# Head order, scaled maxima, the spatial product by seven products of halves, and a new order of pieces in an attention and gating kernel

## Chip, cores and metric

One Trainium2 chip, one core in use. The metric is the device time of one execution in microseconds (us), as the median of several runs. A profiled execution of the kernel before gives the span and the rows below.

## What is computed

```python
scores = concat(where(|i-j| < 16, q@k.T/8, -1e9), q@blockmax(k).T/8 + log(32))
a = softmax(scores);  x = a @ concat(v, blockmean(v))     # 2 batches, 8 heads, 768 x 64; blocks of 32
x = concat_heads(x)                                       # 2 x 768 x 512
gate = sigmoid(causal_conv5(x));  x = (gate * (x @ w_val)) @ w_out
h = relu(x @ w_in)                                        # 512 -> 1024
u, v = h[..., :512], h[..., 512:]
v = (v - mean) / sqrt(var + 1e-6)
out = (u * (w_spatial @ v + b_spatial)) @ w_out2
```

The weights of the last three lines and w_val arrive as 64-bit floats.

## The kernel before

Nearly all the work is fp32 matmuls. Each fp32 operand is held as a high and a low part, and `mm3` (396) multiplies high by high, high by low and low by high: three matmuls per product of 128 x 128 by 384 or 512 columns. The high part is a cast, mostly on ScalarE (ACT), the low part a subtraction, mostly on GpSimd (POOL); `WHO` (32) says which engine does which. `load64` (444) brings a 64-bit weight tile in: one DMA, one ACT `activation` into PSUM and two operations on VectorE (DVE: a shift and a shift-or). `split64` (462) then makes high and low. So each such tile of 128 x 512 costs ACT two instructions.

The program is a list of pieces that `ORDER` (42) names in sequence; a piece can call others that it needs:

- `lk`, `lq`, `lv`, `kw`, `vsum`, `put`: keys, queries, values, windows and block summaries of a pair of heads. `kw` takes the block maxima of the keys on DVE and copies the keys on ACT and POOL.
- `score`, `at`, `pv` (567 to 660), 16 ticks of two heads and half the sequence each. `scores` multiplies, takes minus the row maximum by `tensor_reduce` into `nm` in SBUF, scales `nm` by 0.125 in place, and has ACT do six exponentials with `nm` as bias. `a_T` transposes, and ACT copies into `aT`. `pv` multiplies with v; the two heads write to two halves of the columns of the array. Then ACT copies (`xhi`), DVE subtracts (`xlo`), and the convolution runs over the same PSUM bank: one ACT multiplication (`conv0`), four DVE multiply-adds.
- `gate` (663): one tanh per half sequence and batch (four gates in all). `val` (671): four products by w_val per gate, each followed by a DVE product with the gate, an ACT cast and a POOL subtraction, which give G.
- `wp` (783): w_out by w_in, worked out ahead of the rest in two halves; the weights for the first half are `wout` and `in1`, for the second `in0`.
- `v` (687): 128 rows of the v half, 12 matmuls of 512 columns, relu on ACT, the normalisation on DVE and POOL, high and low parts. `u` (717): the u half.
- `s` (735): the spatial product, 16 pieces (four per half sequence and batch) of 18 matmuls of 384 columns; DVE adds the bias from PSUM and multiplies by u, ACT casts, POOL subtracts. `ws` loads w_spatial.
- `r` (754): 128 rows of the result, 12 matmuls of 512 columns, one ACT copy, one DMA; the last row block goes in two halves of columns.

`Planner` (60) records every instruction of all pieces with what it depends on, sorts them by a table of costs, and issues them per engine in that sequence (`issue`). Every instruction is issued in one place, so the profile puts all on line 190; rows are told apart by the names of tiles (`u` any of 28 general buffers, `ps` PSUM, `a` the scores, `nm` the maxima) and their shapes. Each engine runs its list in sequence and waits at its head.

## Time and profile before

| | us |
|---|---|
| runs, median of 3 (lowest, highest) | 286.23 (285.75, 287.6) |
| the profiled execution, its own time | 283.49 |
| its span in the trace | 281.7 |
| busy: PE, DVE, ACT, POOL | 264.4, 172.9, 160.9, 132.6 |

PE is TensorE, whose granted clock stands at 1.00 in every window. A busy time sums the instructions of an engine; the ends of matmuls are modelled, and a matmul that is drawn longer than the next one's start still counts as busy. The trace shows two matmul records for each instruction of the scores and of the product with v. In a row of windows, the columns are: stretch, its length, then for PE, PEld (weight loads), DVE, ACT and POOL the busy us with the number of instructions, the granted clock, the share of the DMA engines, GB/s.

### The profile page before, as it was taken

What the parts mean: (1) busy time and instruction counts of PE and PEld (TensorE: products, weight loads), DVE (VectorE), ACT (ScalarE), POOL (GpSimd) and SP (SyncE); (2) the same over time, 40 slices, a digit from 0 to 9 for tenths busy, and PEclk for the clock granted to TensorE, in tenths of its full rate; (3) what the DMA queues carried; (4) which work ended last, traced back from release to release, by engine and by line L of the source; (5) the groups of instructions that cost most, each with busy time, mean ns of one, the idle gap of its engine ahead of it and who ended that gap; (6) DMA issues with size and microseconds to landing.
All of it is one profiled execution on the core that took longest, in us unless ns stands there. A gap on an engine that the chain in (4) does not pass through costs nothing.

```text
span 281.7 us, 5411 instructions
## 1 busy us (share of the span) xinstructions
PE 264.4 (94%) x1976; PEld 234.2 (83%) x1976; DVE 172.9 (61%) x394; ACT 160.9 (57%) x440; POOL 132.6 (47%) x166
## 2 busy tenths in 40 slices
PE   0599999999899999999999899999999999999995
PEld 0385677788788998889999889989899989999885
DVE  1897778789979992882489697927595401024000
ACT  3887989999797549869325867534364211211221
POOL 4797673615776275496602634058475500112100
PEclk9999999999999999999999999999999999999999
DMA  6999998889991113430000020002022031000222
GB/s 233 384 409 346 268 250 171 202 216 234 381 258 51 42 24 109 107 100 14 0 2 3 0 77 2 2 0 74 2 74 74 0 114 74 0 2 0 76 80 106
DMA packets 13466, 32.15 MB, mean 114 GB/s; under 512 B 1853, under 2 KB 4448, under 8 KB 13440
## 3 DMA queue, kind: packets, MB, share of 16 engines
q1 hardware_dynamic: 13248, 31.66, 37.3%
q8 instruction: 15, 0.25, 0.4%
q0 software_dynamic: 192, 0.15, 0.2%
q14 instruction: 11, 0.09, 0.1%
HBM read 27.48 MB, written 3.15 MB: 109 GB/s over the span
## 4 chain that ended last, share of the span: by engine, by line
PE 63%; ACT 13%; DMA 8%; DVE 7%; issue 4%; POOL 3%; POOLq 0%; ACTq 0%; DVEq 0%
PE ps L190 63%; ACT a L190 6%; ACT u L190 4%; DMA u<-in_moe_w_out_dram 4%; DVE u L190 3%; DMA u<-in_moe_w_spatial_dram 3%; POOL u L190 2%; ACT aT L190 2%; DMA u<-in_moe_w_in_dram 2%; DVE nm L190 1%; DVE a L190 1%; DVE km L190 1%; ACT ps L190 1%; POOL a L190 1%; DVE st L190 0%
## 5 line engine op out<-in xcount | busy, mean ns | idle before, releaser
L190 PE MATMUL ps<-u,u 128*128 128x384 f32 (+3 forms) x1452 | 232.4, 345 | 10.1 <-ACT u L190 8.9
L190 PEld LDWEIGHTS ps<-u,u 128*128 128x128 f32 (+1 forms) x1452 | 205.4, 200 | 29.8 <-ACT u L190 9.5
L190 POOL TENSOR_TENSOR u<-u,u 128x512 fp32r<-128x512 f32 (+2 forms) x70 | 86.1, 1245 | 90.5 <-ACT u L190 86.6
L190 ACT CAST u<-u 128x384 fp32r<-128x384 f32 (+2 forms) x70 | 39.7, 588 | 35.9 <-DVE u L190 29.8
L190 DVE SCALAR_TENSOR_TENSOR u<-ps,cw,u 128x384 f32<-128x384 f32 (+4 forms) x64 | 37.2, 607 | 1.3 <-ACT u L190 1.2
L190 ACT ACTIVATE u<-ps 128x512 fp32r<-128x512 f32 (+2 forms) x44 | 23.7, 566 | 24.3 <-PE ps L190 24.1
L190 POOL TENSOR_TENSOR a<-a,sm 128x360 f32<-128x360 f32 x32 | 25.7, 822 | 22.7 <-DVE sm L190 17.0
L190 DVE TENSOR_TENSOR gate<-ps,bias 128x384 f32<-128x384 f32 x16 | 8.6, 551 | 36.9 <-PE ps L190 36.9
L190 ACT ACTIVATE a<-a,nm 128x120 f32<-128x120 f32 x48 | 18.4, 393 | 4.9 <-DVE nm L190 3.9
L190 ACT COPY u<-ps 128x512 f32<-128x512 f32 (+1 forms) x13 | 7.2, 555 | 23.0 <-PE ps L190 23.0
L190 DVE TENSOR_SCALAR u<-u 128x512 uint32<-128x512 uint32 (+1 forms) x21 | 14.8, 712 | 8.0 <-DMA u<-in_moe_w_in_dram 5.3
L190 PEld LDWEIGHTS ps<-aT,u 120*64 120x64 f32 x384 | 14.2, 137 | 6.2 <-ACT aT L190 2.9
L190 PE MATMUL ps<-aT,u 120*64 120x64 f32 x384 | 16.1, 225 | 3.5 <-ACT aT L190 1.8
L190 ACT ACTIVATE a<-ps,nm 128x120 f32<-128x120 f32 x48 | 16.9, 362 | 1.4 <-DVE nm L190 0.4
L190 ACT ACTIVATE ps<-u 128x512 f32<-128x512 f32 x20 | 13.0, 650 | 7.9 <-DMA u<-in_moe_w_in_dram 4.0
L190 ACT COPY aT<-ps 120x384 f32<-120x384 f32 x32 | 13.8, 498 | 4.8 <-PE ps L190 4.8
L190 DVE SCALAR_TENSOR_TENSOR u<-ps,u 128x512 uint32<-128x512 uint32 x20 | 13.5, 685 | 1.9 <-ACT ps L190 1.1
L190 DVE BATCH_NORM_STATS2 st<-u 128x6 f32<-128x512 f32 x12 | 8.2, 685 | 10.3 <-ACT u L190 10.2
L190 DVE TENSOR_SCALAR sm<-ps 128x3 f32<-128x3 f32 x32 | 5.1, 158 | 15.2 <-ACT a L190 15.0
L190 PE MATMUL ps<-ident,a 128*120 128x128 f32 x96 | 13.6, 276 | 0.1
L190 PEld LDWEIGHTS ps<-ident,a 128*120 128x120 f32 x96 | 10.8, 137 | 1.8 <-issue 0.5
L190 DVE TENSOR_TENSOR u<-ps,u 128x384 fp32r<-128x384 f32 x16 | 8.6, 550 | 4.9 <-ACT u L190 3.4
(50 smaller groups left out, 184.5 us busy)
## 6 DMA issues: line engine op xcount, KB each, us to landing
u<-in_moe_w_in_dram SPq DMA_DIRECT2D x8, 512.0 KB, 9.8
u<-in_moe_w_out_dram SPq DMA_DIRECT2D x8, 512.0 KB
ks<-in_k_dram SPq DMA_DIRECT2D x8, 384.0 KB, 10.9
u<-in_q_dram SPq DMA_DIRECT2D x8, 384.0 KB
u<-in_vn_dram SPq DMA_DIRECT2D x8, 384.0 KB, 8.4
u<-in_v_dram SPq DMA_DIRECT2D x16, 192.0 KB, 4.7
out_dram<-u SPq DMA_DIRECT2D x11, 256.0 KB, 2.0
u<-in_moe_w_spatial_dram SPq DMA_DIRECT2D x6, 384.0 KB, 3.6
```

Of the source, the lines that this page charges most:

```text
L190: getattr(real, method)(*args, **kw)
```

## The change

1. `ORDER` is rewritten, and some of the planner's costs with it (start of the DMA wire, small bf16 matmuls, which DVE instructions share a port with POOL). A PSUM tile that two engines touch now makes a dependency whatever the addresses.
2. In `pv` each matmul depends on the copies of both heads.
3. The maxima go into spare PSUM columns of the score bank; the scaling reads them there and writes `nm`.
4. In `pv` ACT's reads of the bank are recorded ahead of DVE's.
5. Batch 1's spatial product is done by seven products of halves: the 768 x 768 and 768 x 512 operands are cut in halves, sums of halves are formed, and 14 pieces of nine matmuls of 384 columns take the place of eight of 18. w_spatial is loaded a second time (6 DMAs of 384 KB).
6. Code behind `KSC`, which is 0, goes.

```diff
 ORDER = """
-    in1 wout mask*2 wout in1 wp*2 wout in1 wp in1 in0 wout lk*2 wp in0 wval*2 in0*2 lk kw lk wp lq score vsum lq masks
...
+    mask*2 wout in1*4 wout cw wp*2 wout masks wout in0*3 lk lq wp*2 lq kw lk kw in0 lv vsum lk*2 score put lq kw score
...
-                if (w or writes) and a0 < p1 and p0 < a1 and b0 < f1 and f0 < b1:
+                if name.startswith("ps") and q.eng != eng:
+                    o.deps.add(q)
+                elif (w or writes) and a0 < p1 and p0 < a1 and b0 < f1 and f0 < b1:
                     o.deps.add(q)
...
+        raw = banks[0][:, NI * KW + NI : NI * KW + 3 * NI].rearrange("p (h i) -> p h i", h=2)
         for h in range(2):
-            dve.tensor_reduce(nm[:, h], s3[h], axis=AX.X, op=ALU.max, negate=True)
-        if not KSC:
-            dve.tensor_scalar(nm, nm, 0.125, None, op0=ALU.mult)
+            dve.tensor_reduce(raw[:, h], s3[h], axis=AX.X, op=ALU.max, negate=True)
+        dve.tensor_scalar(nm, raw, 0.125, None, op0=ALU.mult)
...
             copy("at", ATT[t, h], pt)
+            LAST[t, h] = plan.ops[-1]
...
+                    plan.ops[-1].deps.update((LAST[t, 0], LAST[t, 1]))
...
-        copy("xhi", xx[:, 0], x)
-        sub("xlo", xx[:, 1], x, f(xx[:, 0]))
         if g:
             act.copy(xp[:, 0:4], XL[n])
+        copy("xhi", xx[:, 0], x)
...
+        sub("xlo", xx[:, 1], x, f(xx[:, 0]))
         for s in range(1, 5):
...
+    def fast_v(t, h):
+        n = NT // 2
+        if t < n:
+            x = HX[t] = bass.AP(h.tensor, h.offset, [h.ap[0], [1, 768]])
+            dve.tensor_sub(x[:, 512:768], x[:, 256:512], x[:, 0:256])
+            hi, lo = th.get(), th.get()
+            copy("vhi", hi, x[:, 256:768])
+            sub("vlo", lo, x[:, 256:768], f(hi))
+        else:
+            x, y = HX.pop(t - n), bass.AP(h.tensor, h.offset, [h.ap[0], [1, 1280]])
+            dve.tensor_add(y[:, 512:768], x[:, 0:256], y[:, 0:256])
+            dve.tensor_sub(y[:, 768:1024], y[:, 512:768], x[:, 256:512])
+            dve.tensor_sub(y[:, 1024:1280], y[:, 256:512], y[:, 768:1024])
+            hi, lo = unit()[:, 0:1280], unit()[:, 0:1280]
+            copy("vhi", hi, y)
+            sub("vlo", lo, y, f(hi))
+        FV[t] = (hi, lo)
+
+    def fast_t(t):
...
+            sp.dma_start(raw[i], w_sp[(t + i * NT // 2) * P : (t + i * NT // 2 + 1) * P, :])
...
+        dve.tensor_sub(t1, b12, b11)
+        dve.tensor_sub(t2, b22, t1)
+        dve.tensor_sub(t3, b22, b12)
+        dve.tensor_sub(t4, b21, t2)
+        hi, lo = unit(), unit()
+        for i in range(2):
+            cs = slice(2 * i * CH, 2 * (i + 1) * CH)
+            copy("wshi", hi[:, cs], y[:, cs])
+            sub("wslo", lo[:, cs], y[:, cs], f(hi[:, cs]))
+        FT[t] = (hi, lo)
+
+    PRODUCTS = [(x, j) for x in (1, 6, 2, 7, 4, 5, 3) for j in range(2)]
...
+    def fast_s(i):
...
+            for k, (a, c) in enumerate(((0, 0), (0, 1), (1, 0))):
+                pe.matmul(po, A[a], Bs[c], start=first and t == 0 and k == 0, stop=t == n - 1 and k == 2, skip_group_check=True)
+        if x == 1:
+            y = SUM["p", j] = ps_.get().rearrange("p (a s) -> p a s", a=2)
+            for g in range(2):
+                dve.tensor_add(y[:, g], po, bias[:, g * CH : (g + 1) * CH])
+            SUM["e", j] = ps_.get().rearrange("p (a s) -> p a s", a=2)
+        elif x == 6:
+            dve.tensor_add(SUM["e", j][:, 0], po, SUM["p", j][:, 1])
+        elif x == 7:
+            dve.tensor_add(SUM["e", j][:, 1], po, SUM["p", j][:, 1])
+        if x in (1, 6, 7):
+            return
+        g, m, other = {2: (0, 2 + j, bias[:, 0:CH]), 4: (0, j, SUM["p", j][:, 0]), 5: (1, j, SUM["e", j][:, 1]), 3: (1, 2 + j, SUM["e", j][:, 0])}[x]
+        finish_s(b, g, m, po, other, f"f{i}")
```

`finish_s` holds the bias, u, cast and subtraction of the old `spatial`; the first three result blocks of batch 1 need ten of the 14 products, the last three all.

What the rewritten order does on SP, which issues the loads, from the ninth load on. Before:

```order
L190 DMA u_109<-in_moe_w_out_dram 128x1024
L190 DMA ks_78<-in_k_dram 128x768
L190 DMA ks_79<-in_k_dram 128x768
L190 DMA u_115<-in_moe_w_in_dram 128x1024
L190 DMA u_118<-in_moe_w_val_dram 128x1024
L190 DMA u_121<-in_moe_w_val_dram 128x1024
L190 DMA u_124<-in_moe_w_in_dram 128x1024
L190 DMA u_126<-in_moe_w_in_dram 128x1024
L190 DMA ks_80<-in_k_dram 128x768
L190 DMA u_133<-in_q_dram 128x768
L190 DMA u_140<-in_vn_dram 96x1024
L190 DMA u_141<-in_vn_dram 96x1024
```

After, from the sixth:

```order
L195 DMA u_97<-in_moe_w_out_dram 128x1024
L195 DMA u_105<-in_moe_w_out_dram 128x1024
L195 DMA u_109<-in_moe_w_out_dram 128x1024
L195 DMA u_112<-in_moe_w_in_dram 128x1024
L195 DMA u_115<-in_moe_w_in_dram 128x1024
L195 DMA u_118<-in_moe_w_in_dram 128x1024
L195 DMA ks_78<-in_k_dram 128x768
L195 DMA u_120<-in_q_dram 128x768 x2
L195 DMA ks_79<-in_k_dram 128x768
L195 DMA u_128<-in_moe_w_in_dram 128x1024
L195 DMA u_131<-in_v_dram 64x768 x2
L195 DMA u_131<-in_v_dram 16x1472 x2
```

Here `in_moe_w_out` and `in_moe_w_in` are weight tiles of 512 KB, `in_moe_w_val` those of w_val, `ks` a pair's keys, `in_q` its queries. The first keys stand at place 10 before and at 12 now, but the first queries move from place 18 to 13, and the w_val tiles behind the values. Counted over ACT's list, 14 activations and 14 casts of 64-bit tiles and three copies of keys stand ahead of the first exponential before, 12, 11 and two now.

On ACT, between the tanh of the first gate and the last of the four casts (`CAST u_<-u_ 128x384`) that make the high part of G. Before:

```order
L190 COPY ps_269<-xl_202 128x4
L190 CAST u_247<-u_177 128x384 x2
L190 CAST u_250<-u_177 128x384
L190 CAST u_245<-u_244 128x768
L190 COPY aT_266<-ps_265 120x384
L190 COPY aT_268<-ps_267 120x384
L190 CAST u_270<-u_244 128x768
L190 CAST u_242<-ps_269 128x384
L190 ACTIVATE u_243<-ps_269,cw 128x384
L190 ACTIVATE a_257,ps_253<-ps_253,nm_255 128x120 x3
L190 ACTIVATE a_258,ps_254<-ps_254,nm_255 128x120 x3
L190 CAST u_250<-u_177 128x384
```

And now:

```order
L195 COPY aT_247<-ps_246 120x384
L195 COPY aT_249<-ps_248 120x384
L195 CAST u_235<-u_182 128x384 x2
L195 CAST u_238<-u_182 128x384 x2
L195 COPY ps_268<-xl_181 128x4
L195 CAST u_269<-ps_268 128x384
L195 ACTIVATE u_270<-ps_268,cw 128x384
L195 COPY ps_271<-xl_200 128x4
L195 ACTIVATE a_254,ps_250<-ps_250,nm_252 128x120 x3
L195 ACTIVATE a_255,ps_251<-ps_251,nm_252 128x120 x3
L195 CAST u_269<-ps_271 128x384
```

The four casts stood apart, with two casts of w_spatial (128x768) and six exponentials ahead of the last; they now follow one another ahead of the exponentials. DVE's list moves alike: the four products of gate and val stood as three and one, and now stand together.

On PE, the tick of the product with v in which the heads did not take turns, in the stretch behind the first `v` piece (`aT_` numbers are heads; x6 is six in a row). Before:

```order
L190 MATMUL ps_435<-aT_410,u_228 64x64
L190 MATMUL ps_435<-aT_408,u_228 64x64
L190 MATMUL ps_435<-aT_410,u_228 64x64
L190 MATMUL ps_435<-aT_408,u_228 64x64
L190 MATMUL ps_435<-aT_410,u_228 64x64
L190 MATMUL ps_436<-aT_412,u_229 64x64 x6
L190 MATMUL ps_436<-aT_414,u_229 64x64 x6
L190 MATMUL ps_443<-u_245,u_280 128x384 x3
```

And now:

```order
L195 MATMUL ps_467<-u_440,u_222 128x384 x2
L195 MATMUL ps_448<-aT_445,u_442 64x64 x5
L195 MATMUL ps_448<-aT_447,u_442 64x64 x5
L195 MATMUL ps_448<-aT_445,u_442 64x64
L195 MATMUL ps_448<-aT_447,u_442 64x64
L195 MATMUL ps_464<-aT_461,u_442 64x64
L195 MATMUL ps_464<-aT_463,u_442 64x64
L195 MATMUL ps_464<-aT_461,u_442 64x64
```

One tick in that stretch keeps its heads apart in both orders (six and six before, five and five now); all others there take turns in both. Ahead of the first `v` piece 22 matmuls follow one of the same head before, two now.

## Rows read from the trace of the kernel before

**Rows 1.** Four windows (columns: stretch, us, busy us of PE, PEld, DVE, ACT, POOL).

```profile
28.20:62.60 34.40, 33.63 (x368) 25.31 (x367) 27.15 (x69) 31.89 (x115) 18.84 (x32) 1.00 0.91 222
62.60:88.40 25.80, 24.58 (x253) 22.02 (x251) 23.70 (x54) 21.87 (x70) 16.58 (x18) 1.00 0.91 257
88.40:170.50 82.10, 80.28 (x735) 74.81 (x733) 60.29 (x155) 51.95 (x160) 41.94 (x49) 1.00 0.14 41
170.50:278.70 108.20, 108.13 (x565) 99.52 (x564) 42.20 (x90) 35.33 (x67) 34.17 (x34) 1.00 0.12 43
```

**Rows 2.** Two more windows, same columns: to the second gate, and spatial stage.

```profile
5.30:97.90 92.60, 85.47 (x731) 68.81 (x732) 79.70 (x171) 77.81 (x223) 56.66 (x74) 1.00 0.86 252
207.00:249.00 42.00, 42.00 (x225) 39.62 (x224) 12.22 (x25) 12.67 (x24) 12.86 (x12) 1.00 0.16 57
```

**Rows 3.** Groups by form, PE, 170.5 to 278.7 us (count, busy, mean ns).

```profile
L190 PE MATMUL ps<-u,u 128*128 128x384 f32 x336 | 59.5, 335 | 0.1
L190 PE MATMUL ps<-u,u 128*128 128x512 f32 x204 | 47.2, 390 | 0.0
```

**Rows 4.** Timeline of ACT (start us, us, instruction, count [idle before]).

```profile
5.29 0.64 ACT L190 ACTIVATE ps<-u 128x512 f32<-128x512 f32 x1 [3.27 <-DMA u<-in_moe_w_in_dram]
...
33.75 0.35 ACT L190 ACTIVATE a<-ps,nm 128x120 f32<-128x120 f32 x1
...
74.54 0.83 ACT L190 CAST u<-u 128x768 fp32r<-128x768 f32 x1 [1.03 <-DMA u<-in_moe_w_spatial_dram]
...
80.51 0.52 ACT L190 CAST u<-u 128x384 fp32r<-128x384 f32 x1
...
270.41 0.59 ACT L190 COPY u<-ps 128x512 f32<-128x512 f32 x1 [2.13 <-PE ps L190]
273.13 0.59 ACT L190 COPY u<-ps 128x512 f32<-128x512 f32 x1 [2.13 <-PE ps L190]
```

**Rows 5.** Timeline of DVE: a scaling of maxima, and products of gate and val.

```profile
33.06 0.16 DVE L190 TENSOR_SCALAR nm<-nm 128x6 f32<-128x6 f32 x1
...
71.42 1.48 DVE L190 SCALAR_TENSOR_TENSOR u<-u,ps 128x384 f32<-128x384 f32 x3
...
79.83 0.55 DVE L190 SCALAR_TENSOR_TENSOR u<-u,ps 128x384 f32<-128x384 f32 x1
...
97.93 0.56 DVE L190 SCALAR_TENSOR_TENSOR u<-u,ps 128x384 f32<-128x384 f32 x1
```

**Rows 6.** Timeline of PE: the first v half, then products with v.

```profile
81.08 2.36 PE L190 MATMUL ps<-u,u 128*128 128x512 f32 x11
...
119.36 0.92 PE L190 MATMUL ps<-aT,u 120*64 120x64 f32 x24
...
154.98 2.31 PE L190 MATMUL ps<-aT,u 120*64 120x64 f32 x60
158.08 0.91 PE L190 MATMUL ps<-aT,u 120*64 120x64 f32 x12 [0.79 <-ACT aT L190]
```

**Rows 7.** Groups by form, whole span (count, busy us, mean ns).

```profile
L190 POOL TENSOR_TENSOR u<-u,u 128x512 fp32r<-128x512 f32 x32 | 43.1, 1355 | 27.5 <-ACT u L190 23.8 <-POOL u L190 1.8 <-DMA ks<-in_k_dram 1.7
...
L190 ACT CAST u<-u 128x512 fp32r<-128x512 f32 x32 | 19.6, 618 | 8.8 <-DVE u L190 8.5
...
L190 ACT ACTIVATE a<-ps,nm 128x120 f32<-128x120 f32 x48 | 16.9, 362 | 1.4 <-DVE nm L190 0.4
...
L190 ACT ACTIVATE ps<-u 128x512 f32<-128x512 f32 x20 | 13.0, 650 | 7.9 <-DMA u<-in_moe_w_in_dram 4.0 <-DMA u<-in_moe_w_out_dram 2.9 <-DMA u<-in_moe_w_val_dram 0.6
L190 POOL TENSOR_TENSOR u<-u,u 128x768 fp32r<-128x768 f32 x6 | 11.1, 1843 | 2.8 <-ACT u L190 2.7
...
L190 DVE TENSOR_TENSOR u<-gate,u 128x384 f32<-128x384 f32 x16 | 9.3, 594 | 0.5
...
L190 ACT COPY u<-ks 128x768 f32<-128x768 f32 x8 | 6.7, 842 | 2.0 <-POOL u L190 2.0
...
L190 DVE TENSOR_SCALAR nm<-nm 128x6 f32<-128x6 f32 x16 | 5.7, 357 | 0.0
```

More of the change, by code (lines that the diff above doesn't have):

```diff
@@ L171, in cost @@
             one = method in ("tensor_copy", "tensor_scalar") and not psum and not out_psum
-            lock = one or len(sbuf_in) > 1
+            lock = one or len(big) > 1 or n == 1 and not psum
             ptr = sum(1 for x in args[2:5] if hasattr(x, "ap") and size(x) == 1) if method != "tensor_tensor" else 0
@@ L733, in tile_kernel, with finish_s @@
     yh = Parts(768)
+    def finish_s(b, g, m, po, other, name):
+        yy = Y[b, g, m] = yh.get().rearrange("p (a s) -> p a s", a=2)
+        u = U[b, m][:, g * CH : (g + 1) * CH]
+        gt = att([P, CH], "gate", f"gate{name}")
+        dve.tensor_add(gt, po, other)
+        eng("ymul").tensor_mul(u, gt, u)
+        copy("yhi", yy[:, 0], u)
+        sub("ylo", yy[:, 1], u, f(yy[:, 0]))
     def spatial(i):
+        if i >= (B - 1) * NC * KT:
+            return fast_s(i - (B - 1) * NC * KT)
         (b, g), m = divmod(i // KT, NC), i % KT
@@ L839, in tile_kernel @@
         "wp": w_product(), "val": each(B * NC * KT, val), "v": each(B * NT, vhalf), "u": each(B * NC * KT, uhalf),
-        "ws": w_spatial(), "out2": split64("out2", w_out2, 0), "s": each(B * NC * KT, spatial), "r": each(B * NT, result)}
+        "ws": w_spatial(), "out2": split64("out2", w_out2, 0), "wt": each(NT // 2, fast_t), "s": each((B - 1) * NC * KT + 14, spatial), "r": each(B * NT, result)}
     count = {name: 0 for name in threads}
```

96 lines of the change are left out of this document (59 added, 37 removed).

## The prediction

> **What bounds the kernel now.** I read the windows first. In the last 108.2 us PE is busy for 108.13 and is never starved [rows 1]: there each matmul taken away is time taken away. From 88.4 to 170.5 it is busy for 80.28 of 82.1, from 28.2 to 88.4 for 58.2 of 60.2. This last figure flatters it, since a matmul that has to wait is drawn long. Counting pitch shows the starving: result blocks of 12 matmuls come 273.13 − 270.41 = 2.72 us apart [rows 4], 0.227 us per matmul of 512 columns. The 336 of 384 columns then share 108.2 − 204 × 0.227 = 61.9 us with the 25 others of that window [rows 1, 3]; as half of a 512 each, these take 2.8, which leaves 0.176 us per matmul of 384. Ahead of the first v half, which starts at 81.08 [rows 6], stand 104 matmuls of 512 columns (23.6 us by this pitch), 48 of 384 (8.4), six ticks of the product with v at 0.9 [rows 6], nine of scores, taken as long (together 13.5), and transposes and masks, which I estimate by their columns at 9: some 55 us. About 26 us of PE are lost there, and only some 5 behind it. Next I looked at who makes PE wait: from 28.2 to 62.6 ACT is busy for 31.89 of 34.4, from 62.6 to 88.4 DVE for 23.70 of 25.8 [rows 1]. So the head of the program is bound by the lists of ACT and DVE, the rest by PE.
>
> **The head, by the new order.** The same matmuls stand ahead of the first v half in both orders, by kind and count, so the change there is the waiting. ACT works through its list from 5.29, reaches the first exponential at 33.75 and the fourth cast of G at 80.51 [rows 4]; PE follows at 81.08.
> Ahead of the first exponential go two activations, three casts and a copy of keys: 2 × 0.650 + 3 × 0.618 + 0.842 = 4.0 us [rows 7]. A 20-wide operation that moves ahead takes back some 0.2. That is −3.8 us.
> From there to the fourth cast, six exponentials leave (at least 0.362 each, 2.2; with the read of the sum behind each, nearer 3), a cast of w_spatial (0.83 [rows 4]) and two casts and two multiplications of a PSUM bank (about 2.0, taken like the 0.52 of the last cast). In come two activations, three casts and two copies of keys, 1.3 + 1.85 + 1.68 = 4.8 us [rows 7]: the splits of w_val, which were only put off. Together −0.2 to −1; I take −1.
> So ACT gives −4.8 us at the first v half. DVE allows as much: its fourth product of gate and val starts 79.83 − 71.42 = 8.4 us after the first, three of which take 1.48 [rows 5]. The four now stand together, so nearly 7 us of other work move behind them. I take −5.0 us. The bounds: nothing, if the put-off work is late for the next gate; and −7.7 at the top. That top comes from DVE. Its list up to the fifth product (97.93 [rows 5]) holds the same work in both orders within 1 us. In that stretch DVE is busy for 79.70 of 92.6 us [rows 2], so without its 12.9 idle us the second gate could come 12.9 earlier. Were it to keep them all, PE could run only through the two further v halves that now stand ahead of the second gate's; some 18 us of waiting would remain of the 26.
>
> **Maxima scaled out of PSUM.** The scaling takes 0.16 us at 33.06 but 0.357 in the mean [rows 5, 7], so some wait. If the PSUM form never waits, 16 × 0.2 = 3.2 us of DVE go; if it takes as long as the SBUF form, none. The exponentials waited 1.4 us on `nm` in one of their two groups [rows 7]. This is inside the head's range; I add nothing.
> The Trainium skill, page SBUF — State Buffer, section Who interferes with whom, says that DVE and GpSimd share one pair of SBUF ports as an exclusive lock, and that a DVE instruction with two SBUF inputs contends with GpSimd's reads. The trace agrees for the scaling in so far as its mean is twice its shortest. By the rule in full the scaling would save the 3.2 us of DVE in the head, and each of the 24 DVE sums that item 5 adds between two SBUF operands could wait as long in the last third, 24 × 0.2 = 4.8 us, where DVE is idle for 66 of 108 us: the sum would stay within 1 us, and the chance of the third rival rises a little.
>
> **Heads that take turns.** A tick with turns takes 0.92 us for 24 records. The lone second half of one took 0.91 for 12, after a wait of 0.79 for `aT` [rows 6]. Turns are worth 0.07 us per instruction of the list. But 20 of the 22 places gained lie ahead of the first v half, where PE waits anyway. Behind it ten become eight: −0.1 us. The added wait for both copies comes first: the first head's matmuls wait for a second copy of at most 0.5 us, 8 ticks there, 4 us if nothing were queued between. PE's list puts other matmuls ahead, so I take 0, and keep +1 for the range.
>
> **ACT first on the bank.** DVE's subtraction goes behind an ACT multiplication, some 0.5 us, 16 times. DVE's 12.9 idle us in the head [rows 2] cover it: 0. If the order of the two lists fails to cover, 8 ticks × 0.5 = 4 us come off the head's gain, which its lower bound holds. The removed `KSC` code emitted nothing.
>
> **Seven products of halves.** 8 × 18 = 144 matmuls become 14 × 9 = 126 of the same width, in PE's saturated window: 18 × 0.176 = −3.2 us. The cover for what is added:
> - DVE: 12 sums of 384 columns and eight more on the way out at 0.594, 12 of 256 at two thirds of it: 7.1 + 4.8 + 4.8 = 16.7 us [rows 7].
> - POOL: six subtractions of 768 at 1.843, and three of 1280 (1.843 × 1280/768 = 3.07) for three of 512 (1.355): 11.1 + 5.1 = 16.2 us.
> - ACT: scaled from 0.618 by columns, 6 × 0.93 + 3 × 0.93 = 8.4 us.
> From 207 to 249 these three are busy for 12.2 to 12.9 of 42 us [rows 2], and in the whole window for 34 to 42 of 108 [rows 1]. All that is added fits twice. What counts is lateness at two places. After the last v half of batch 1 POOL's list holds about 20 us (two of 512, three of 1280, four of 768, two powers) plus some 5 us for DVE and ACT ahead of it; PE's list holds 34 us of matmuls before it needs the last of these. At the end the last product's sum, multiplication, cast and subtraction (0.59 + 0.59 + 0.52, and 1.355 × 384/512 = 1.02) take 2.7 us, and 16 matmuls of 0.227, 3.6 us, stand between. Both hold; if one fails by a step it costs 1 to 3 us. I take +0.4.
>
> **Sum.** −5.0 − 0.1 − 3.2 + 0.4 = −7.9 us. The span goes from 281.7 to 273.8; with the 1.79 around it (283.49 − 281.7) the profiled execution would take 275.6. It stood 1% below the median of the runs (286.23/283.49 = 1.0097), so the median after is 278.3 us, −2.8%. A measurement of this kernel can tell about 1% (2.9 us) from no change.
>
> **Rivals.**
> 1. *The gain in the head is given back.* The w_val splits and the key copies are only put off, and DVE's work to the second gate is the same. If PE starves at that gate, only −3.2, −0.1 and +0.4, and perhaps −0.8 of the head, stay: 281.7 − 3.7 = 278.0, with the same two steps 282.5 us. For it: DVE's 23.70 of 25.8 us [rows 1]. Against it: two more v halves and the u pieces now stand ahead of that gate. Chance 0.20, about 0.12 of it past 1%.
> 2. *The head gives all it can*, −7.7, and DVE saves its waits too, −1: 281.7 − 12.0 + 0.4 = 270.1, on the median's scale 274.5 us. For it: ACT and DVE both lose work ahead of the first v half, and POOL is busy for only 16.58 of 25.8. Chance 0.20.
> 3. *Slower: POOL is late for the products of sums.* The place is PE's wait for the low parts of 1280 and 768 columns. POOL's queue of 20 us must stretch: by 9 us (34 − 25) before PE waits at all, by 17 before the gain of 7.9 is gone, by 20 before it is 1% slower. At twice its length, 20 + 20 + 5 − 34 = 11 us of waiting: 278.3 + 11.4 = 289.7 us. For it: 24 DVE instructions with two SBUF inputs beside it, and means that depend on the neighbours (0.16 against 0.357). Against it: 12.9 busy of 42 us [rows 2]. Chance 0.05; a milder form, within 1%, 0.02.
> 4. *The turns do nothing*: that is already in my sum, since ten places become eight.
>
> **How the numbers follow.** My own case (head −3 to −7, 276 to 280.5 us) has 0.53. Faster by over 1%: 0.53 + 0.20 + 0.12 = 0.85. Within 1%: 0.08 of rival 1, 0.02 of rival 3, rounded to 0.10. Slower by over 1%: 0.05. The range goes from the middle of rival 2 with a part of its own error, 272, to beyond rival 1, 284.5.
>
> **What would show it.** First exponential near 29 to 30 us instead of 33.75; first v half near 76 instead of 81.08; PE's window from there to the end full, as before, and 3.2 us shorter; no wait of PE on POOL of more than 1 us between the spatial products; DVE, ACT and POOL busier by 17, 8 and 16 us in the last third without PE noticing. I am wrong if the second gate's v halves come no earlier than before, if PE waits in the spatial stage, or if the first exponential comes late because the queries land later than their new place says.

## The result, and the profile after

The kernel after takes 287.91 us (median of 20 runs, 285.02 to 289.56), the kernel before beside it 284.4 (20 runs). The ratio is 1.0108, with a 95% interval of 1.0078 to 1.0139: 1.1% slower, where 2.8% faster was forecast. The profiled execution takes 286.44 us, its span 284.7 where that of before was 281.7.

The four windows of the kernel after, with the columns of [rows 1]:

```profile
28.20:62.60 34.40, 29.26 (x303) 21.21 (x301) 26.34 (x65) 27.68 (x103) 14.67 (x21) 1.00 0.92 227
62.60:88.40 25.80, 24.48 (x268) 22.14 (x265) 21.07 (x50) 22.40 (x70) 17.18 (x22) 1.00 0.71 210
88.40:170.50 82.10, 80.10 (x721) 74.43 (x720) 59.01 (x156) 54.30 (x166) 44.46 (x50) 1.00 0.17 50
170.50:278.70 108.20, 105.56 (x573) 95.58 (x574) 66.01 (x132) 40.66 (x73) 51.65 (x40) 1.00 0.21 71
```

In the first window ACT is busy for 27.68 us instead of 31.89 [rows 1], but PE did less there too: 303 matmul records instead of 368. In a window of fixed length a busy time also falls when the engine waits more, so this is no sign yet of a shorter list. In the last window PE, full before, stands still for 2.6 us.

A better measure is ACT from its first instruction to the end of the fourth cast of G, in two stretches that meet at the first exponential (same columns). Before:

```profile
5.29:33.75 28.46, 23.23 (x105) 16.14 (x106) 23.25 (x35) 23.50 (x42) 20.54 (x23) 1.00 1.03 362
33.75:81.03 47.28, 45.38 (x496) 36.91 (x494) 41.00 (x102) 42.31 (x152) 27.65 (x40) 1.00 0.94 241
```

and after:

```profile
4.03:29.82 25.79, 19.17 (x112) 13.89 (x112) 18.92 (x30) 20.04 (x37) 18.91 (x25) 1.00 1.01 327
29.82:79.45 49.63, 43.16 (x458) 34.18 (x456) 38.22 (x89) 40.85 (x137) 25.88 (x36) 1.00 0.86 228
```

ACT is busy for 60.9 us instead of 65.8, 4.9 less, and idle for 14.5 instead of 9.9, 4.6 more.

To put all on one scale I add up PE's lost time: the start of a matmul less the undisturbed time of all matmuls ahead of it (0.227 us for 512 columns, 0.173 for 384, the others likewise), worked out from PE's timeline of the profiled executions. The columns are the times, in us, by which it was lost.

| lost by | 40 | 55 | 80 | 100 | 200 | end | matmuls alone |
|---|---|---|---|---|---|---|---|
| before | 15.6 | 19.0 | 23.3 | 23.7 | 29.1 | 29.0 | 249.4 |
| after | 16.7 | 21.8 | 25.0 | 26.6 | 33.4 | 34.9 | 246.3 |

The matmuls are 3.1 us shorter, the loss 5.9 longer: 2.8, nearly the whole 3.0 of the span. Of the 5.9, 2.9 had come by 100 us, 1.4 more by 200, and 1.6 behind that.

ACT around the first exponential, and from the wait for w_spatial to the four casts of G [rows 4]:

```profile
29.82 0.36 ACT L195 ACTIVATE a<-ps,nm 128x120 f32<-128x120 f32 x1 [0.19 <-DVE nm L195]
...
72.48 0.84 ACT L195 CAST u<-u 128x768 fp32r<-128x768 f32 x1 [2.11 <-DMA u<-in_moe_w_spatial_dram]
...
75.43 1.49 ACT L195 ACTIVATE u<-u 128x1536 f32<-128x1536 f32 x1
...
77.60 1.85 ACT L195 CAST u<-u 128x384 fp32r<-128x384 f32 x4
```

The first exponential comes 3.9 us earlier, and the four casts stand in a row, both as read from the lists. But the fourth cast ends at 79.45 instead of 81.03 us: of the 3.9 us, 1.6 are left there. ACT's wait of 2.11 us for w_spatial took little of them, since DVE's convolution ahead of the tanh at 75.43 ends only at 74.83. PE has nothing of them:

```profile
80.12 12.59 PE L195 MATMUL ps<-u,u 128*128 128x512 f32 x84
```

In the kernel before, the first v half does not start at 81.08, as [rows 6] and the prediction have it. A row of the timeline puts matmuls of the same tiles together, whatever their width, and the row of 16 at 77.02 holds seven of 384 columns and then, from 78.35, the first nine of the v half:

```profile
77.02 3.57 PE L190 MATMUL ps<-u,u 128*128 128x384 f32 x16
80.43 0.82 PE L190 MATMUL ps<-ident,a 128*120 128x128 f32 x6
```

Counted by form from 77.03 to 80.43 us:

```profile
L190 PE MATMUL ps<-u,u 128*128 128x512 f32 x9 | 2.2, 393 | 0.0
```

Only the last three of the twelve, which need the fourth cast, stand behind the transposes, from 81.08. So the first v half starts 1.8 us later now (80.12 against 78.35), and its last matmul 0.4 us later (82.76 against 82.35). That agrees with the lost time by 80 us, 1.7 us more.

ACT's waits from 30 to 66 us (what waited, for what, us, how often, longest), after:

```profile
ACT a L195 <- DVE nm L195: 4.5, 3, 2.9
ACT u L195 <- PE ps L195: 0.9, 2, 0.6
ACT ps L195 <- DMA u<-in_moe_w_val_dram: 0.6, 1, 0.6
```

and before:

```profile
ACT u L190 <- PE ps L190: 1.5, 3, 0.9
ACT a L190 <- DVE nm L190: 0.4, 1, 0.4
ACT u L190 <- DVE u L190: 0.3, 1, 0.3
```

6.0 us instead of 2.2. For part of this, DVE's maxima wait for PE's scores, and PE's own timeline shows why these come late:

```profile
40.11 0.50 PE L195 MATMUL ps<-u,minus 128*128 128x512 f32 x1 [0.77 <-ACT u L195]
40.55 0.82 PE L195 MATMUL ps<-u,u 64*64 64x120 f32 x16
...
44.73 2.92 PE L195 MATMUL ps<-u,u 64*64 64x120 f32 x31 [1.59 <-DMA u<-in_q_dram]
...
51.95 0.51 PE L195 MATMUL ps<-u,minus 128*128 128x512 f32 x1 [1.40 <-ACT u L195]
52.39 0.81 PE L195 MATMUL ps<-u,u 64*64 64x120 f32 x16
```

A matmul by `minus` belongs to `wp`: ACT multiplies a finished product by 0.5 for its high part (`act.mul(hi, po, 0.5)`), PE then takes that away in PSUM. 16 matmuls of scores (64x120) stand behind it on PE. On ACT the multiplication for the one at 51.95 (the line at 51.31) stands behind exponentials that wait for DVE:

```profile
48.67 0.36 ACT L195 ACTIVATE a<-ps,nm 128x120 f32<-128x120 f32 x1 [2.87 <-DVE nm L195]
...
51.31 0.59 ACT L195 ACTIVATE u<-ps 128x512 fp32r<-128x512 f32 x1
```

So there is a ring in the order of the lists: exponentials wait for maxima, maxima for scores, scores for a `minus` matmul, and this for a multiplication behind exponentials. But the longest of ACT's waits, the 2.87 us at 48.67, is none for scores. DVE's list ahead of it:

```profile
45.84 0.16 DVE L195 TENSOR_SCALAR sm<-ps 128x3 f32<-128x3 f32 x1 [0.72 <-ACT a L195]
...
46.15 1.14 DVE L195 TENSOR_REDUCE ps<-ps 128x3 f32<-128x360 f32 x2
47.20 1.29 DVE L195 TENSOR_TENSOR u<-u 96x512 f32<-96x512 f32 x1
48.41 0.15 DVE L195 TENSOR_SCALAR nm<-ps 128x6 f32<-128x6 f32 x1
```

DVE waits for the sums of ACT's last exponentials, takes two maxima without a wait for PE, does a block sum of the values (96x512), and only then scales. The kernel before has block sums of 2.85 us at such a place, behind the maxima at 36.64, and ACT did not wait for that scaling: it had a key copy and five multiplications of `wp` in its list there. So work that the new order takes out of ACT's list between exponentials had also covered waits. No run moves the block sum or gives ACT other work in that place.

In the last third of the kernel after, PE's longest waits: one for the last pair's values, and two for ACT, which waits for POOL:

```profile
175.27 1.40 PE L195 MATMUL ps<-aT,u 120*64 120x64 f32 x31 [1.44 <-DMA u<-in_v_dram]
...
191.45 28.39 PE L195 MATMUL ps<-u,u 128*128 128x512 f32 x138 [0.27 <-ACT u L195]
220.68 1.50 PE L195 MATMUL ps<-u,u 128*128 128x384 f32 x7 [0.84 <-ACT u L195]
```

with POOL's subtractions ahead of them,

```profile
187.20 3.65 POOL L195 TENSOR_TENSOR u<-u,u 128x768 fp32r<-128x768 f32 x2 [2.17 <-DVE u L195]
...
217.07 4.17 POOL L195 TENSOR_TENSOR u<-u,u 128x1280 fp32r<-128x1280 f32 x2 [2.13 <-ACT u L195]
```

and ACT between POOL and PE (a cast, and a relu of the u half, which waits for POOL until 220.0):

```profile
190.89 3.41 ACT L195 CAST u<-u 128x384 fp32r<-128x384 f32 x8 [2.87 <-POOL u L195]
...
220.03 0.60 ACT L195 ACTIVATE u<-ps 128x512 f32<-128x512 f32 x1 [2.53 <-POOL u L195]
```

### The profile page after: what moved, and what is told of

Same layout as the page of the kernel before. It is cut to its first block, busy times and chain, and to the rows that moved or that the text cites. A ratio compares the mean times of both kernels' runs of the same rounds, so it can differ in the third digit from the quotient of the medians.

```text
span 284.7 us, 5456 instructions
## 1 busy us (share of the span) xinstructions
PE 259.7 (91%) x1958; PEld 228.7 (80%) x1958; DVE 190.0 (67%) x426; ACT 166.2 (58%) x446; POOL 149.3 (52%) x172
## 4 chain that ended last, share of the span: by engine, by line
PE 53%; DMA 21%; ACT 9%; DVE 7%; POOL 5%; issue 2%; SPq 1%; POOLq 0%; DVEq 0%; ACTq 0%
PE ps L195 53%; DMA u<-in_moe_w_in_dram 6%; ACT a L195 5%; DMA u<-in_v_dram 5%; DVE u L195 4%; POOL u L195 4%; ACT u L195 4%; DMA u<-in_moe_w_val_dram 4%; DMA u<-in_moe_w_spatial_dram 3%; DMA u<-vm 3%; SPq L195 1%; DVE ps L195 1%; DVE a L195 1%; POOL a L195 1%; ACT aT L195 0%
## 5 line engine op out<-in xcount | busy, mean ns | idle before, releaser
L195 PE MATMUL ps<-u,u 128*128 128x384 f32 (+3 forms) x1434 | 229.8, 346 | 16.1 <-ACT u L195 12.2
L195 PEld LDWEIGHTS ps<-u,u 128*128 128x128 f32 (+1 forms) x1434 | 201.3, 200 | 38.3 <-ACT u L195 14.0
L195 POOL TENSOR_TENSOR u<-u,u 128x384 fp32r<-128x384 f32 (+3 forms) x76 | 102.5, 1364 | 90.5 <-ACT u L195 80.0
L195 ACT CAST u<-u 128x384 fp32r<-128x384 f32 (+3 forms) x76 | 45.8, 636 | 46.0 <-DVE u L195 34.4
L195 DVE SCALAR_TENSOR_TENSOR u<-ps,cw,u 128x384 f32<-128x384 f32 (+3 forms) x64 | 37.0, 607 | 0.0
L195 ACT ACTIVATE u<-ps 128x512 fp32r<-128x512 f32 (+2 forms) x44 | 23.5, 565 | 20.7 <-PE ps L195 16.6
L195 DVE TENSOR_TENSOR u<-u 128x384 f32<-128x384 f32 (+5 forms) x28 | 17.9, 650 | 0.2
L195 PE MATMUL ps<-aT,u 120*64 120x64 f32 x384 | 13.8, 225 | 1.6 <-DMA u<-in_v_dram 1.4
L195 DVE TENSOR_TENSOR u<-ps,u 128x384 fp32r<-128x384 f32 (+1 forms) x20 | 10.9, 552 | 5.0 <-ACT u L195 4.0
L195 DVE TENSOR_TENSOR u<-u,u 128x384 f32<-128x384 f32 (+2 forms) x16 | 14.0, 889 | 0.1
L195 DVE TENSOR_TENSOR gatef<-ps,u 128x384 f32<-128x384 f32 x6 | 3.3, 557 | 15.2 <-PE ps L195 15.2
```

What stands on the lines that cost most here:

```text
L195: getattr(real, method)(*args, **kw)
```

## Experiments

"Lists kept" below means that every engine gets the very sequence of the named kernel, and only what the edit names differs; the others are planned anew. The diffs are shortened to what they do. A ratio is to the kernel before that ran beside. Lost times are on the scale of the table above.

### The parts alone

**plain_tail**: the kernel after, batch 1's spatial product as before.

```diff
-        if i >= (B - 1) * NC * KT:
-            return fast_s(i - (B - 1) * NC * KT)
-    ... val*3 v*3 out2 v out2 v*2 u*3 wt*2 u s*2 u*3 s out2 u s*5 r*6 s*2 r*3 s*4 r*3
+    ... val*3 v*3 out2 v out2 v*2 u*4 s*2 out2 s r*5 s u*4 s*4 r*7
```

> The changed kernel with batch 1's spatial product as it was before (eight pieces of 18 matmuls, no second load of w_spatial); the order ahead of it, the turns, the maxima and the PSUM rule stay. Theory A (the new order of loads starves the head, and the seven products do their 3.2 us): 144 matmuls stand where 126 stood, so about 3 us slower than the changed kernel, ratio to before 1.018 to 1.024. Theory B (the seven products cost more in waiting, through POOL and the general buffers, than the 18 matmuls are worth): faster than the changed kernel, ratio 0.995 to 1.008, and PE without a wait of over 0.5 us behind 170 us.

287.58 us, ratio 1.0116 (1.0077 to 1.0156), between the two expectations. The seven products change nothing that the intervals of some 1.1 us show: 3.1 us of matmuls against 2.3 of waiting in the profiles (32.6 us lost, not 34.9). And with none of them the loss is whole. The wait for the last pair's values is there without them too, 1.00 us instead of 1.44:

```profile
175.48 1.99 PE L194 MATMUL ps<-aT,u 120*64 120x64 f32 x48 [1.00 <-DMA u<-in_v_dram]
```

**only_seven**: the kernel before with `fast_s` and what it needs, its tail in the sequence of after.

```diff
-    pv*3 out2 s*2 at*3 pv*3 gate val*4 v*2 gate val*4 u v*4 u*3 out2*2 s*2 out2 s r*5 s u*4 s*4 r*7
+    pv*3 out2 s*2 at*3 pv*3 wt gate val*4 v*2 gate val*4 u v*4 u*3 wt*2 out2*2 s*2 u*3 s out2 u s*5
+    r*6 s*2 r*3 s*4 r*3
```

> The kernel before with the seven products alone: old order, old rules and costs, old reads of the banks; only the end of the order has its new pieces. Theory A: the matmuls saved come out nearly whole, ratio 0.988 to 0.995. Theory B: the waits eat them, ratio 0.998 to 1.012, with PE waiting on POOL or on a load of v between 165 and 230 us.

295.49 us, ratio 1.04 (1.0345 to 1.0455), far above both expectations. Between 225 and 255 us PE waited 5.5 us for POOL in two waits, the longest 3.0, and 2.4 for ACT in two: rival 3's mechanism, in an order that gives it less cover.

**only_parts**: parts 2 to 4 and the planner's rules and costs, with the order of before. **neworder_only**: the reverse, the code and costs of before with the order of after (plain tail).

> The kernel before with the turns, the maxima in PSUM, ACT first on the bank, the PSUM rule and the planner's costs; old order of pieces, old spatial product. Theory C (the added dependencies on PSUM tiles cost waits of their own): ratio above 1.005. Theories A and B: 0.993 to 1.003, the scaling of maxima at 0.17 us throughout instead of 0.357 in the mean.

> The kernel before with the new order of pieces alone (its tail as before, no seven products, no turns, maxima in SBUF, old costs of the planner, so the lists are planned anew). If the order is what loses in the head, the loss is there without the other parts: 288 to 294 us, ratio 1.015 to 1.035. If the order is good and the other parts of the change lose, it is 280 to 284 us.

only_parts takes 292.34 us, ratio 1.026 (1.0206 to 1.0314); neworder_only 300.2, ratio 1.0542 (1.0458 to 1.0626). By 85 us PE has lost 30.3 and 30.2 us, where before and after lose 23.5 and 25.3. Neither half stands alone. I read this as order and costs fitting each other, but nothing here shows it: both are planned anew, the added dependencies on PSUM tiles (theory C) are not tested apart, and of what only_parts loses by 85 us some 3 are the clock's (0.64 in 65 to 70 us, 0.68 in 70 to 75). neworder_only, slower still than it was expected to be, loses another 14 us behind 85.

**held_max** and **held_turns**: the kernel before, lists kept, with the maxima in PSUM, or with the heads taking turns behind the later of the two copies.

```diff
-            dve.tensor_reduce(nm[:, h], s3[h], axis=AX.X, op=ALU.max, negate=True)
-        dve.tensor_scalar(nm, nm, 0.125, None, op0=ALU.mult)
+            dve.tensor_reduce(raw[:, h], s3[h], axis=AX.X, op=ALU.max, negate=True)
+        dve.tensor_scalar(nm, raw, 0.125, None, op0=ALU.mult)
```

> The kernel before, every engine's list kept instruction by instruction, but the 16 pairs of row maxima are written to the spare PSUM columns and scaled from there. Theory D (the scaling out of PSUM saves the waits on the SBUF form): its mean falls from 0.357 us to about 0.17, 3 us of DVE time, of which PE sees at most 1: ratio 0.996 to 1.000. Theory C (PSUM costs a dependency or a slower access): ratio above 1.003.

> The kernel before, every list kept, but the 12 matmuls of each tick of the product with v are put in turns behind the later of the two copies. My prediction: worth nothing or 0.1 us, since the places gained lie where PE waits anyway: ratio 0.998 to 1.002. Rival: the head is bound by PE too, all 22 places count at 0.07 us, 1.5 us: ratio 0.994 to 0.997. Other rival: the first head's matmuls now wait for the second copy: 1.003 or more.

held_max: 284.77 us, ratio 1.002 (0.9988 to 1.0053), no change. Its scaling never waits now, which is what the sum took for possible and valued at nothing (group of DVE by form, [rows 7] has 357 ns):

```profile
L198 DVE TENSOR_SCALAR nm<-ps 128x6 f32<-128x6 f32 x16 | 2.4, 150 | 0.0
```

held_turns: 284.91 us, ratio 1.0045 (1.0017 to 1.0072): slightly slower. PE's waits for `aT` are 1.9 us in two, the longest 1.4, against 1.8 and 1.0: the added wait, if anything, outweighs the turns.

### The head

**queries_first**: the kernel after with keys and queries ahead of values in `ORDER`, planned anew. **held_queries**: lists kept, only SP's loads move.

```diff
-        kw in0 lv vsum lk*2 score put lq kw score wp at wp kw wval vsum score lq score lv*2
+        kw in0 lk*2 lq*2 lv vsum score put kw score wp at wp kw wval vsum score score lv*2
```

> The changed kernel with the loads of the third and fourth pair's keys and queries named ahead of the first pair's values and of the block sums. Theory A: the fourth query no longer lands at 44.6 us but before 38, PE's lost time by 55 us falls from 21.8 by 2 to 3 us, ratio 0.998 to 1.006. Theory B: the head improves too, but the lost time is taken back by 100 us, and the ratio stays 1.008 to 1.014.

> The changed kernel, all lists kept but SP's: the third pair's keys and the queries of pairs 3 and 4 are loaded ahead of the first pair's values and block sums. Theory A (PE and ACT starve on loads that the new order puts behind): the wait for a query at 44.7 us goes, PE's lost time by 55 us falls from 21.8 by 1.5 to 3 us, and the whole by 1 to 2 us: ratio to before 1.003 to 1.008. If the gain is taken back by the gate (which needs all four pairs and w_val): 1.009 to 1.013.

288.87 us (1.0106 to 1.0233) and 287.09 (1.0079 to 1.016). The wait of 1.59 us for the query went and another came for it:

```profile
42.19 0.79 PE L203 MATMUL ps<-u,minus 128*128 128x512 f32 x1 [1.58 <-ACT u L203]
```

**cut_loads_after, cut_loads_before**: both kernels, lists kept, with eight weight loads cut to an eighth. POOL fills the rest of the tile with zeros, so seven eighths of these weights are left out.

```diff
-                sp.dma_start(raw, src)
+                sp.dma_start(raw[:, 0:128], src[:, 0:128])
+                pool.memset(raw[:, 128:], 0)
```

> The kernel after, every list kept, with an eighth of the bytes of eight weight loads (the four tiles of w_in for the second half of wp and the four of w_val: 64 KB in place of 512 KB each); GpSimd fills the rest of each tile with zeros (eight memsets of about 0.8 us), so these weights are left out of the result. If it is the loads that take the head's gain of 5 us, this gives it back: ScalarE waits for VectorE and DMA in the head as little as in the kernel before, the first v half starts 4 us or more ahead of that of the kernel before with the same cut, and the median is 2 to 5 us below that kernel's. If ScalarE, VectorE and PE wait for each other's results whatever the loads, the first v half comes within 1.5 us of the other's and this kernel stays 2 to 4 us slower than it.

> The kernel before with the same cut of the same eight loads, every list kept: the other half of the pair. If loads hold the kernel before as well, it gains as much as the kernel after, 3 to 6 us; if its head is bound by the lists of ScalarE and VectorE, as the prediction had it, it gains less than 2 us: 281.5 to 283.5 us.

288.66 us (1.0057 to 1.0196) and 287.19 (1.0009 to 1.0098): neither gains. In the kernel after the DMA share fell from 1.04 and 0.99 to 0.54 and 0.30 in 35 to 45 us,

```profile
35.00:40.00 5.00, 4.47 (x29) 2.81 (x28) 4.43 (x9) 4.70 (x12) 4.54 (x8) 1.00 0.54 128
40.00:45.00 5.00, 5.00 (x54) 3.69 (x54) 3.54 (x8) 3.20 (x13) 0.88 (x4) 1.00 0.30 68
```

and the head stayed as it was: the wait for the query went, the `minus` matmul took its time, and ACT still waited 4.5 us for the maxima.

```profile
51.60 0.51 PE L205 MATMUL ps<-u,minus 128*128 128x512 f32 x1 [3.07 <-ACT u L205]
...
81.06 6.14 PE L205 MATMUL ps<-u,u 128*128 128x512 f32 x48
```

The longest wait for maxima, of 2.87 us, is unchanged though no query is waited for; DVE's list ahead of it is the one shown above:

```profile
48.32 0.36 ACT L205 ACTIVATE a<-ps,nm 128x120 f32<-128x120 f32 x1 [2.88 <-DVE nm L205]
```

With memsets of 0.83 us on POOL in their place, then, the loads alone do not give the gain back. (The kernel before became slower under its memsets: its first v half went from 78.35 to 87.24 us in an execution at a mean clock of 0.971, so the pair says nothing on the difference, and a cost of the memsets in the kernel after isn't ruled out.)

**held_hi_first**: the kernel after, lists kept but ACT's: each `act.mul(hi, po, 0.5)` directly behind its product. **held_hi_queries**: with SP's move of held_queries as well. ACT, at the place of 51.31 us:

```diff
+ACTIVATE u_184<-ps_183 128x512
 ACTIVATE a_175,ps_171<-ps_171,nm_173 128x120 x3
 ACTIVATE a_176,ps_172<-ps_172,nm_173 128x120 x3
 ACTIVATE vm_164<-u_162 96x128
-ACTIVATE u_184<-ps_183 128x512
```

> The kernel after, every list kept but ScalarE's: the multiplications that make the high parts of wp, for which PE's matmuls by minus wait, stand directly behind their last product instead of behind exponentials and copies (five places; in the largest, at 51.95 us, six exponentials move behind one). Nothing is left out. If the head's gain is lost in a ring of waits (ScalarE's exponentials wait for VectorE's maxima, these for PE's scores, PE for a high part that stands behind exponentials on ScalarE), PE's three waits of 0.5, 0.8 and 1.4 us for ScalarE between 34 and 55 us go, PE has lost 19 to 20.5 us by 55 us instead of 21.8, and the median is 285 to 286.5 us, 1 to 2.5 below the kernel after. If the waits only move, as with the queries, it is 287 to 288.5 us.

> The same, and on SyncE the keys and queries of pairs 3 and 4 ahead of the first values, as in the run with the queries alone (287.09 us). In that run the wait for the query (1.6 us) went and a wait for ScalarE grew in its place, and when eight loads were cut a wait of 3.1 us for the high part of wp did. If that ring is what kept both from paying, here both waits go: PE has lost 17.5 to 19.5 us by 55 us (before: 19.0), the first v half starts at 77 to 79 us instead of 80.1, and the median is 283.5 to 285.5 us. If something else sets the head, it is 286.5 us or more.

held_hi_first: 286.65 us, ratio 1.0066 (1.0027 to 1.0106), 1.3 below after but 0.15 above the expected range, and the intervals overlap. PE's wait for ACT's `u` in the head fell to 0.5 us, waits for DVE of 0.7 and 0.6 came for it, and ACT's longest wait for maxima is still 2.31 us. The clock of that profile is 0.50 from 55 to 65 us, so it says nothing on the first v half. held_hi_queries: 288.6 us, ratio 1.0157 (1.0101 to 1.0213), against its expectation. In its profile the first v half does come earlier than in after, as expected, though not than in before (78.35),

```profile
78.61 6.14 PE L207 MATMUL ps<-u,u 128*128 128x512 f32 x48
```

and PE has lost 1.5 us less than after by then, since the same matmuls stand ahead; by 115 us both have lost 26.7. The gain is given back ahead of the second gate: at 85.89 PE waits 1.14 us for ACT, which it does not in after. This profile's clock is 0.87 and 0.79 in 50 to 60 us, and ACT still waits 2.33 us for the maxima in question.

### The granted clock

Over the runs the mean granted clock differs. Of the 20 of after, five at 0.993 or above took 285.0 to 286.6 us, nine at 0.976 or below 288.1 to 289.6. The kernel before, in the 106 runs that stood beside the experiments, had 0.998 or more in 68 (median 283.7), the kernel after in three of 20. At 0.993 or more the median is 283.9 for before (85 runs) and 286.4 for after (five): as far as five runs tell, some 2.5 us of the 3.5 between the medians are left without the clock. Profiles at a lower mean show where the clock goes: here held_no_lows (below), whose head has the lists of after,

```profile
50.00:55.00 5.00, 3.69 (x48) 2.88 (x48) 2.76 (x8) 4.11 (x14) 1.53 (x2) 0.82 0.94 270
55.00:60.00 5.00, 5.00 (x53) 3.61 (x53) 4.24 (x13) 4.67 (x18) 0.35 (x1) 0.50 1.07 243
60.00:65.00 5.00, 5.00 (x32) 3.64 (x24) 4.44 (x14) 4.69 (x22) 1.73 (x5) 0.65 0.91 305
65.00:70.00 5.00, 5.00 (x68) 4.88 (x68) 3.75 (x7) 4.40 (x15) 3.96 (x5) 1.00 1.01 375
```

0.50 is 1.2 GHz, and it comes with a stretch in which PE stood idle for 1.3 of 5 us. The idle time there doesn't decide it alone: the profile of after has 1.4 idle us in the same 5 and keeps 1.00.

**held_warm**: the kernel after, lists kept, with 14 repeated matmuls ahead of PE's waits between 34 and 52 us.

```diff
+            for _ in range({("wp", 5): 2, ("score", 3): 3, ("wp", 6): 6, ("score", 4): 3}.get(piece, 0)):
+                pe.matmul(*args, **{**kw, "stop": True})
```

> The kernel after, every list kept, with 14 repeated matmuls on PE (two and six of 512 columns, three and three of 360, each the first matmul of a group that overwrites its bank) ahead of the four places between 34 and 52 us where PE waits 0.5 to 1.8 us. Nothing is left out, and the repeats take about 3.3 us, most of it inside those waits. If PE's idle stretches there let the granted clock fall later in the head, most runs come with a clock of 0.99 or more and the median falls to 285 to 286.5 us in spite of the added work. If the clock falls for another reason, the runs keep clocks of 0.976 to 0.988 and the median is 287.5 to 290 us.

All ten runs had a clock of 0.992 or more, where the four of held_lows_dve (below), beside them with PE's list of after, had 0.976 to 0.988. So PE's idle stretches between 34 and 52 us do have a part in bringing the clock down. The profile at 55 to 65 us reads

```profile
55.00:60.00 5.00, 4.52 (x63) 3.53 (x60) 4.91 (x15) 4.83 (x18) 1.09 (x2) 1.00 1.08 280
60.00:65.00 5.00, 4.88 (x63) 4.02 (x61) 4.54 (x14) 4.74 (x24) 2.13 (x5) 1.00 0.98 336
```

The time was 287.53 us all the same, ratio 1.0122 (1.0088 to 1.0155): about 1 us above the five runs of after with such a clock, so what the clock gave back, the repeats seem to have taken; their price was not measured by itself. That miss of the expectation limits the clock's part: it goes with differences of up to 3 us between runs of the kernel after, but it isn't the whole loss.

### The seven products

**held_no_lows** and **held_no_lows_all**: the kernel after, lists kept, memsets on POOL in place of the six subtractions of 768 columns and the three of 1280. The low parts of the sums are left out. Both names stand for the same kernel, run in two sets: the second text takes the first run for one with the subtractions of 768 columns alone, which no run has, and it counts twelve and four where there are six and three.

```diff
-            sub("vlo", lo, y, f(hi))
+            pool.memset(lo, 0.0)
...
-            sub("wslo", lo[:, cs], y[:, cs], f(hi[:, cs]))
+            pool.memset(lo[:, cs], 0.0)
```

> The changed kernel, all lists kept, but POOL's subtractions that make the low parts of the sums (six of 768, three of 1280 columns) are memsets; the low parts of these operands are left out of the result. Theory B by POOL (rival 3 of the prediction): PE's lost time behind 186 us, 2.8 us in the changed kernel, falls by 1.5 to 2.5, ratio to before 1.002 to 1.006. If the general buffers and the loads are the cause: no change behind 186 beyond 0.5 us, ratio 1.008 to 1.013.

> The kernel after, every list kept, with memsets in place of all subtractions on GpSimd that the sums brought: the twelve of 768 columns for w_spatial and the four of 1280 columns for the last v half (left out of the result: the low parts of these sums). The bound for all that GpSimd can have cost in the seven products. By the run without the twelve alone (285.02 us) it is 284.5 to 285.2 us; if the rest of the loss too were GpSimd's, it is 282.5 to 283.5 us.

285.02 us, ratio 1.0054 (1.0024 to 1.0083), and 285.61, ratio 1.0014 (0.9973 to 1.0055; that set's before stood at 285.39). PE has no wait left behind 186 us and loses 0.7 us there instead of 2.8. So POOL's nine subtractions are behind those two waits, but DVE gains as well. Its six sums of 384 columns that read two SBUF operands, in the kernel after and in held_no_lows:

```profile
L195 DVE TENSOR_TENSOR u<-u,u 128x384 f32<-128x384 f32 x6 | 6.7, 1124 | 0.0
```

```profile
L198 DVE TENSOR_TENSOR u<-u,u 128x384 f32<-128x384 f32 x6 | 3.3, 550 | 0.0
```

**held_lows_dve**, and once more beside held_no_lows_all as **held_lows_dve_2**: the six of 768 columns on DVE, the three of 1280 still on POOL, nothing left out. Expected as for twelve.

```diff
-            sub("wslo", lo[:, cs], y[:, cs], f(hi[:, cs]))
+            dve.tensor_sub(lo[:, cs], y[:, cs], f(hi[:, cs]))
```

> The kernel after, every list kept, except that the twelve subtractions of 768 columns that make the low parts of the sums of w_spatial are issued on VectorE at their places in the sequence, not on GpSimd. Nothing is left out. If late low parts from GpSimd cost the seven products their gain (the memset run gave 285.02 us, 1.0054 of before, with 2 us less PE waiting behind 186 us), this gives 284.8 to 285.8 us, ratio 1.005 to 1.008, and no PE wait on GpSimd behind 186 us. If what the memset run saved was GpSimd's contention with the others and not its lateness, VectorE takes the work at a price of its own: 286.5 to 288 us.

> The kernel after, every list kept, with the twelve subtractions of 768 columns for w_spatial on VectorE, run beside the one without any of them, since the first measurement (287.58 us, four runs) had an interval of 1.6 per cent. If late low parts were the cost: 285 to 286 us. If VectorE, which now does them, delays what it did before by as much: 286.8 to 288 us.

287.58 us (1.0023 to 1.0184) and 287.43, ratio 1.0076 (1.0037 to 1.0116). PE loses 1.8 to 1.9 us behind 186 us, and one wait is left there, for ACT, as in the kernel after,

```profile
220.37 4.80 PE L198 MATMUL ps<-u,u 128*128 128x384 f32 x26 [0.84 <-ACT u L198]
```

This is the wait behind the subtractions of 1280 columns, which were not moved; the one of 0.27 us behind those of 768 is gone. By the ratios, leaving nine subtractions out gives 1.5 and 2.7 us, moving six to DVE 0.1 and 0.9. DVE is no idler either: from 170.5 to 278.7 us it is busy for 66.01 us in the kernel after, POOL for 51.65. So it isn't settled how much of the cost is POOL's lateness and how much the work as such; a run with only the three moved or left out is missing.

**seven_dve**: the kernel before with the seven products, these lows on DVE, and a newly sought sequence of pieces behind the spatial stage of batch 0; meant to beat both kernels.

```diff
-    pv*3 out2 s*2 at*3 pv*3 gate val*4 v*2 gate val*4 u v*4 u*3 out2*2 s*2 out2 s r*5 s u*4 s*4 r*7
+    at s*2 at pv*3 wt val out2 v val*4 v*3 gate v u val u val*2 wt u out2 u out2 v gate u s wt s u*2 s u s*3
+    r s r*2 s*5 r s r out2 s r*7
```

> The kernel before with the seven products alone, its order kept up to the spatial stage of batch 0, the pieces behind it put in a new sequence, and the low parts of the sums of w_spatial made on VectorE. If the seven products lose only to late low parts and to the order around them, this is the first version with their gain of 3.2 us less 1: 281.5 to 283.5 us, ratio 0.99 to 1.0. If the sums themselves do not fit beside the v halves, the wait moves to another engine and it is 285 to 290 us.

286.47 us, ratio 1.0088 (1.0043 to 1.0133). The wait moved to ACT:

```profile
233.52 6.77 PE L192 MATMUL ps<-u,u 128*128 128x512 f32 x19 [4.31 <-ACT u L192]
```

None of the versions beats the kernel before.

## Why the prediction was wrong

**The step that failed** is "The head, by the new order": −5.0 us by ACT's list, with DVE's allowing as much. What it read from the lists was right: the first exponential at 29 to 30 us (29.82), the four casts together, ACT's work up to the fourth cast 4.9 us less (4.8 were counted). What it did with them was not. It took an engine that was busy for 31.89 of 34.4 us for the bound and its instructions for the price, as if PE and DVE would follow. In the new lists ACT waits 4.6 us more up to that cast, 3.8 of them from 30 to 66 us and chiefly for maxima, so the cast ends 1.6 us earlier, not 4.8. And PE did not follow the cast: the prediction took 81.08 us for the start of the first v half, when nine of its twelve matmuls had run from 78.35 on. (The 26 us of PE that it counts as lost ahead are some 23 by that.) The first v half now starts 1.8 us later, not 5 earlier, and PE has by then lost 1.7 us more than before.

Why ACT waits is shown in part. The profile has a ring of in-order lists, and in it a wait of 2.9 us that DVE's own list makes. Breaking the ring at the `minus` matmuls alone moved the median by 1.3 us, not beyond the intervals, and with the earlier queries not at all; DVE's link stood in all these runs (2.3 to 2.9 us). The query and the `minus` matmuls are thus shown to be not enough by themselves, and so, but for the memsets, are the loads; what would give the 5 us back stays open.

**Rival 1**, the gain in the head given back, with a chance of 0.20, came nearest, but in outcome more than in mechanism. It had PE starve at the second gate. The fifth product of gate and val, for that gate, does start at 107.11 us instead of 97.93 [rows 5], with two further v halves ahead; but from 100 to 115 us PE loses no more than 0.2 us. The gain was never there to be given back.

**The seven products**: the term −3.2 was right as matmuls (318 records of 384 columns instead of 336, 3.1 us). The term +0.4 for their cover was mis-sized: plain_tail makes it about 3 on the median, with an error of over 1, and 2.3 in the profiles. The count of POOL's work held (subtractions of 768 and 1280 columns at 1.95 and 3.05 us, taken as 1.84 and 3.07). What I had not priced is that the wait reaches PE through a third engine: ACT's cast and relu wait for POOL, at 190.9 and 220.0 us, long before the last product needs its low parts. The wait of 1.44 us for the last pair's values, issued at 169.26 us, is only in small part theirs: 1.00 of it stands in plain_tail too and comes with the order, a cost that the sum had at nothing. Rival 3 had the mechanism, though PE's waits are put down to ACT; in the order of only_seven the loss is of its size, with 5.5 us of it in waits for POOL.

**Maxima, ACT first**: the first gave nothing, as taken; the second was in no run by itself. The rule of the Trainium skill that I weighed (SBUF — State Buffer, section Who interferes with whom) has DVE and GpSimd share one pair of SBUF ports as an exclusive lock, and a DVE instruction with two SBUF inputs contend with GpSimd's reads. The traces agree with it: out of PSUM the scaling takes 0.15 us in the mean instead of 0.357, and the six sums of 384 columns with two SBUF operands take 1.12 us in the mean, not the 0.594 I priced, but 0.55 where memsets stand for POOL's subtractions. The scaling's gain did not move the time (held_max). What the slower sums cost is not shown: the two that POOL waited for, 2.17 us ahead of 187.20, took 0.55 us each. **Turns**: −0.1 and +1 as the end of the range; alone they cost 0.45%, some 1.3 us, so the end was the nearer value. Behind the first v half nothing shows them.

**The range** of 272 to 284.5 us missed, because its slow end held only rival 1 with the seven products' full gain. It had no case in which the head itself becomes worse, nor one in which the clock falls in most runs.

## What to carry to other kernels

A shorter list on the busiest engine is a gain only if what its next instruction waits for comes earlier too: follow the chain, from exponential to maximum to whatever stands ahead of it on VectorE, to score and to whatever stands ahead of the score on PE, before counting instructions. Work that is moved out of a list may have covered a wait there. A row of a merged timeline is not the start of a piece: count the matmuls in it by width first. Where every engine runs its list in sequence, taking one wait away showed the next one four times here, so price a reorder by the chain and let the lists' sums be its upper bound. And added work on an idle engine is covered only if the engines between it and the bound don't wait for its buffers or results.
